# A branch hint, an earlier flag read and stores by thirds at the end of a fused RWKV and SwiGLU kernel

## The chip, the core and the metric

The kernel runs on one core of a Trainium2 chip. A core has five engines that work side by side: TensorE (PE, matrix products; its weight loads are listed as PEld), VectorE (DVE), ScalarE (ACT), GpSimd (POOL) and SyncE (SP, which here only issues transfers and waits). Each engine runs its own instruction queue in order; the queues meet through semaphores. The metric is device time in microseconds, and the median over several executions is what counts.

## The reference

The program computes two things in a row, in float32. The first is a linear attention with a decaying state; the second is a gated feed-forward layer on its output. Shapes: batch 4, 8 heads, 768 steps, head size 48; then 3072 tokens of 384 values, with an inner size of 1536.

```python
for t in range(S):
    kt, vt, rt = (k[:, :, t], v[:, :, t], r[:, :, t])
    cur = np.einsum('bhd,bhe->bhde', u[None] * kt, vt)
    y[:, :, t] = np.einsum('bhd,bhde->bhe', rt, state + cur)
    state = w[None, :, :, None] * state + np.einsum('bhd,bhe->bhde', kt, vt)
...
g = x @ w_gate                       # x: y as (3072, 384)
silu = g * (1.0 / (1.0 + np.exp(-g)))
val = x @ w_val
return silu * val @ w_out
```

## The kernel before, in words

The program holds two whole implementations. `fast` is correct as long as all decay rates `w` lie in a range that its tables of powers can hold; `general` works for any `w`. `fast` runs first and always to its end. On the way (step 12 of its main loop) it counts the entries of `w` outside the range into one integer in on-chip memory, `outside`. The outermost function then reads that integer into a register of every engine (line 1360) and branches (line 1361): if it is over zero, `general` computes everything again and overwrites the output. With the data used here the count is zero, so every engine jumps over the whole of `general`, whose instructions lie between the branch and the end of the program. Behind the branch stand the closing waits: SP waits for every outstanding transfer and every engine, and a barrier over all engines ends the program (put down to line 1755).

`fast` handles 24 blocks of 128 tokens. The attention of a block and the feed-forward of earlier blocks are interleaved by a hand-written order (`todo`, `feed`), and the kernel is built with a manual schedule, so program order on each engine is the order in which the Python code issues. The feed-forward is done for groups of blocks. For the last two groups of four blocks, called by their first pair's number as `THREES` = 8 and `THREES + 2` = 10, the products go through a scheme that multiplies 3 x 3 blocks by 2-column blocks with 15 products instead of 18: `three_units` for the gate and value products (line 787 issues their matmuls) and `project_thirds` for the output projection (line 1013). Everything that remains once the interleaved queue is empty is the list `tail`: the gate and value products of group 8, its projection, the same products of group 10, and its projection. The tail's first matmuls run at 429.8 us.

`project_thirds(g)` has 15 rounds, named r0 to r14 in the order of `THIRDS`, which ends with r2, r6, r9, r5, r11, r7. A round is one matrix product of eight matmuls (two token blocks q of 128 rows, four each) into a PSUM bank, followed by `evict`, which copies, adds or subtracts the bank into one or two of the six result pieces `c[0]` to `c[5]`. The pieces lie in `rows`, which holds, for each q, two output tiles j of 384 columns: piece k is columns 128 (k // 2) to 128 (k // 2) + 128 of tile j = k % 2. The last four rounds finish the pieces: r9 finishes c[4], r5 finishes c[0] and c[1], r11 finishes c[2] and c[3], r7 finishes c[5]. In the last group (`ends`) the two rounds r6 and r7 of the chain "l5" are `split`: each q has a bank of its own and is evicted on its own, on VectorE (line 1008).

`store(q, j)` (line 977) sends one output tile of 128 rows by 384 columns, 192 KB, to DRAM (line 981). It issues from ACT's queue, except in the last group for q = 0, where it issues from SP's. Each transfer raises one of eight counters in turn when it lands; a later transfer on the same counter first waits for the earlier one.

Of the kernel before, what the change touches and what calls it, by code (L numbers as in the profile page):

```python
# [15 lines left out]
P = 128  # L16
# [6 lines left out]
def fast(  # L23
# [24 lines left out]
    nc = tc.nc  # L48
# [7 lines left out]
    DM, DFF = moe_w_gate.shape  # L56
# [41 lines left out]
    def take():  # L98
        return free.popleft()
# [170 lines left out]
    for e in range(2):  # L270
# [3 lines left out]
        out=ub.rearrange("p h d -> p (h d)"),  # L274
        in_=bass.AP(tensor=u.tensor, offset=u.offset, ap=[[0, P], [1, H * D]]),
# [9 lines left out]
    def warm(n):  # L285
# [9 lines left out]
        out=mask[:], in_=mask[:], compare_op=ALU.is_gt, fill=0.0,  # L295
# [11 lines left out]
    for l in range(7):  # L307
        n = 1 << l
# [449 lines left out]
    def prepare_threes(g, n):  # L758
        if n == 6:
            x_forms(g)  # L760
        for _ in range(2):
            if todo_x:
                todo_x.popleft()()
        if g > THREES:
            return
        if n == 1:
            if g == FIRST:
                todo_forms.extend(in_place(0) + in_place(1))
            if g == THREES:
                todo_forms.extend(w_forms(g, 1))  # L770
        if n == 7:
            todo_forms.extendleft(reversed(w_forms(g, 0)))
        for _ in range(2):
            if todo_forms:
                todo_forms.popleft()()
# [127 lines left out]
    def third(x, k, j):  # L903

        return x[:, :, 4 * k : 4 * k + 4, P * j : P * j + P]
# [39 lines left out]
    def project_thirds(g):  # L945

        ends = g + 2 == N // 2
        A, B_, C, D_, E, F = room["h"]
        (x00, x01), (x10, x11), (x20, x21) = (
            [third(hTs, k, j) for j in range(2)] for k in range(3)  # L950
        )
        h = {
            "r3": A, "r4": B_, "r1": C, "r0": D_, "r8": E, "r10": F, "r14": A, "r13": B_,
            "r12": C, "r2": D_, "r6": E, "r5": x00, "r7": x21, "r9": x20, "r11": x11,
        }
        rows = hv[:, NR + 6 : NR + 12].rearrange("p (q r) t -> p q (r t)", q=2)
        c = [rows[:, :, DM * (k % 2) + P * (k // 2) :][:, :, 0:P] for k in range(6)]
        made = {
            0: [(dve.tensor_sub, E, x01, x11)],
            1: [(dve.tensor_add, F, x01, x21)],  # L960
            2: [(dve.tensor_add, A, x10, x20)],
            3: [(dve.tensor_sub, B_, x00, F)],
            4: [(dve.tensor_add, C, B_, x20)],
            5: [(dve.tensor_sub, D_[q], D_[q], x20[:, q]) for q in range(2)],
            6: [(dve.tensor_add, E[:, q], D_[q], x21[:, q]) for q in range(2)],
        }
        used = {
            "r3": [("copy", 2)], "r4": [("copy", 1)], "r1": [("copy", 0)], "r0": [("sub", 2)],
            "r8": [("copy", 3), ("sub", 1)], "r10": [("copy", 5)], "r14": [("copy", 4)],
            "r12": [("add", 0)], "r13": [("add", 4)], "r2": [("add", 5)], "r6": [("add", 3)],  # L970
            "r9": [("sub", 4)], "r5": [("sub", 0), ("sub", 1)], "r11": [("add", 2), ("add", 3)],
            "r7": [("add", 5)],
        }
        lasts = ("r4", "r0", "r8", "r9", "r5", "r11", "r7")
        open_ = {}

        def store(q, j):
            cc, b = divmod(2 * (g + q) + j, B)
            n0 = S * b + P * cc
            issue = sp if ends and q == 0 else act  # L980
            issue.dma_start(out=out[n0 : n0 + P, :], in_=rows[:, q, DM * j : DM * j + DM])

        def make(n):
            for op, o, a, b in made.get(n, ()):
                op(o, a, b)
            if not ends:
                prepare_threes(g + 2, n)

        def item(n):
            what, chain = THIRDS[n]  # L990
            if n:
                make(n)
            first = chain not in open_
            split = ends and chain == "l5"
            if first:
                open_[chain] = [take()] + ([ring_a.popleft()] if split else [])
            banks_ = open_[chain]

            def evict(q):
                for how, k in used[what]:  # L1000
                    x = banks_[0][:, 0 : 2 * P].rearrange("p (q t) -> p q t", q=2)
                    if split:
                        x = banks_[q][:, q * P : q * P + P]
                    o = c[k][:, q] if split else c[k]
                    if how == "copy":
                        act.copy(o, x)
                    else:
                        (dve.tensor_add if how == "add" else dve.tensor_sub)(o, o, x)

            for q in range(2):  # L1010
                ps = banks_[q if split else 0][:, q * P : q * P + P]
                for f in range(4):
                    pe.matmul(  # L1013
                        ps, (h[what][q] if h[what] is D_ else h[what][:, q])[:, f, :], wide["o"][what][:, f, :],
                        start=first and f == 0 and (split or q == 0), stop=f == 3, skip_group_check=True,
                    )
                if split:
                    evict(q)
                    if what == "r7":
                        store(q, 1)  # L1020
            if not split:
                evict(None)
            if n == 0:
                for do in wide.pop("last"):
                    do()
                make(0)
            if what in lasts:
                free.append(banks_[0])
            if what == "r11":
                store(0, 0)  # L1030
                store(1, 0)
            if what == "r7" and not split:
                store(0, 1)
                store(1, 1)
        return [lambda n=n: item(n) for n in range(15)]

    def three_units(g):
# [225 lines left out]
    for s in range(4, N + 2):  # L1263
# [3 lines left out]
        if s + 2 == SWAPPED:  # L1267
# [3 lines left out]
            for p, o in ((slice(0, 64), 64), (slice(64, P), -64)):  # L1271
                sp.dma_start(
                    out=halves_of[p], in_=scales[p.start + o : p.stop + o, 1:3, H // 2 : H]
# [68 lines left out]
    tail = threes[0] + projections[0][:-2]  # L1342
    tail += threes[1][0:1] + projections[0][-2:-1] + threes[1][1:2] + projections[0][-1:]
    tail += threes[1][2:] + projections[1]
    for piece in tail:
        piece()


@with_exitstack
def kernel(  # L1350
    ctx: ExitStack,
    tc: tile.TileContext,
    *args: bass.AP,
):
    nc = tc.nc
    ctx.enter_context(tc.manual_schedule())
    flag = ctx.enter_context(tc.tile_pool(name="flag", bufs=1))
    outside = flag.tile([1, 1], INT32, name="outside")
    fast(tc, *args, outside[:])
    n = nc.values_load(outside[:], min_val=0, max_val=512)  # L1360
    with tc.If(n > 0):
        general(tc, *args)


# [395 lines left out]
```

## Time and profile before

| what | us |
|---|---|
| median of 5 runs | 596.67 |
| lowest and highest of them | 595.38 and 597.52 |
| the profiled execution's own time | 595.54 |
| its span, first to last instruction | 593.8 |
| start of the tail on PE | 429.8 |
| last store issued | 588.1 |
| SP's waits for stores end | 592.2 |

The span is the time from the first to the last instruction of the program; the execution's own time is a little longer, since it holds what the runtime does around it. Busy times are sums per engine, and engines overlap. A wait names the engine that waits, the line, and who released it. The granted TensorE clock in this execution was 0.999 of full speed. A q behind an engine's name means an entry of its instruction queue that is not arithmetic: a transfer's issue, a semaphore wait, a register load, a branch.

### The profile page before, as it was taken

How to read it: one execution, taken by the hardware profiler on the slowest of the kernel's cores; microseconds unless marked ns; L12 is line 12 of the kernel's file. 1: busy time of each engine (PE TensorE's matmuls, PEld its weight loads, DVE VectorE, ACT ScalarE, POOL GpSimd, SP SyncE). 2: the span in 40 equal slices, each digit the busy share in tenths (PEclk: the TensorE clock that was granted, in tenths of full speed). 3: DMA queues.
4: the chain of work that ended last, by engine and by line, in shares of the span. 5: the costliest groups of instructions: out<-in, count | busy, mean ns of one | idle time of the engine just before them, and what ended most of it. 6: DMA issues, size and time to landing. Idle time of an engine off the chain costs nothing.

```text
span 593.8 us, 13239 instructions
## 1 busy us (share of the span) xinstructions
PE 580.6 (98%) x5240; PEld 522.5 (88%) x5240; DVE 421.5 (71%) x702; ACT 225.2 (38%) x516; POOL 355.5 (60%) x378
## 2 busy tenths in 40 slices
PE   8899999999999999999999999999999999999995
PEld 7688888899888899988899988889988899988895
DVE  5977877488488877478787477779257878377672
ACT  3468886221443422244431344423134320233310
POOL 5889879999999502977600996513678960010600
PEclk9999999999999999999999999999999999999999
DMA  7989896952342333233234233200100000100001
GB/s 160 254 220 249 219 298 88 84 80 46 78 75 31 50 54 66 49 54 63 41 57 79 68 53 57 47 13 3 54 1 1 1 1 1 55 0 1 1 2 59
DMA packets 148151, 41.73 MB, mean 70 GB/s; under 512 B 138480, under 2 KB 141936, under 8 KB 148080
## 3 DMA queue, kind: packets, MB, share of 16 engines
q1 hardware_dynamic: 144912, 36.47, 31.1%
q10 hardware_dynamic: 3168, 4.33, 2.0%
q8 instruction: 43, 0.70, 0.5%
q14 instruction: 28, 0.23, 0.1%
HBM read 28.51 MB, written 4.72 MB: 56 GB/s over the span
## 4 chain that ended last, share of the span: by engine, by line
PE 88%; POOL 3%; DVE 2%; issue 1%; ACT 1%; POOLq 0%
PE bank L787 31%; PE bank L606 18%; PE ring L787 13%; PE bank L1013 9%; PE bank L531 7%; PE ring L493 6%; PE ring L440 3%; POOL wgv L242 1%; PE ring L508 1%; DVE hv L811 1%; POOL hats L332 0%; POOL rk L254 0%; POOL hats L329 0%; PE ring L371 0%; POOL rk L255 0%
## 5 line engine op out<-in xcount | busy, mean ns | idle before, releaser
L811 DVE TENSOR_TENSOR hv<-hv,bank 128x512 f32<-128x512 f32 x132 | 87.2, 682 | 25.7 <-PE bank L787 14.6
L531 PE MATMUL bank<-xT,wgv 128*128 128x256 f32 x288 | 66.5, 384 | 0.6 <-ACT xT L497 0.6
L787 PE MATMUL bank<-xf,wgv 128*128 128x256 f32 x256 | 65.9, 382 | 0.0
L350 ACT ACTIVATE At<-ident,du 128x128 f32<-128x128 f32 x176 | 59.9, 398 | 15.0 <-DVE du L260 6.6
L811 ACT COPY hv<-bank 128x512 f32<-128x512 f32 x72 | 40.2, 586 | 58.3 <-PE bank L787 51.9
L531 PEld LDWEIGHTS bank<-xT,wgv 128*128 128x128 f32 x288 | 53.3, 190 | 8.9 <-ACT xT L497 0.9
L717 POOL TENSOR_TENSOR s<-wgv 128x256 f32<-128x256 f32 x39 | 29.9, 791 | 48.6 <-PE bank L606 48.5
L787 PEld LDWEIGHTS bank<-xf,wgv 128*128 128x128 f32 x256 | 47.8, 190 | 7.0 <-DVE kT L1055 0.6
L1064 POOL TENSOR_TENSOR hv<-At,hats 128x512 f32<-128x512 f32 x8 | 10.2, 1274 | 65.9 <-ACT At L1063 65.9
L818 ACT ACTIVATE hv<-hv 128x512 f32<-128x512 f32 (+1 forms) x33 | 21.2, 668 | 45.9 <-DVE hv L811 45.9
L521 POOL TENSOR_TENSOR Z<-Z,w 48x192 f32<-48x192 f32 x32 | 16.9, 528 | 35.7 <-DVE Z L520 34.5
L493 PE MATMUL ring<-At,v_ld 128*32 128x128 f32 x768 | 34.9, 273 | 1.4 <-DVE At L450 1.4
L787 PE MATMUL bank<-xT,wgv 128*128 128x256 f32 x144 | 35.9, 382 | 0.3 <-DVE hv L811 0.3
L787 PE MATMUL bank<-xT,s 128*128 128x256 f32 x152 | 35.3, 380 | 0.0
L606 PE MATMUL bank<-wt,hs 128*128 128x192 f32 x192 | 33.7, 328 | 0.6 <-DVE hs L580 0.6
L606 PE MATMUL bank<-wo,hs 128*128 128x192 f32 x192 | 33.9, 327 | 0.0
L606 PE MATMUL bank<-wo,hv 128*128 128x192 f32 x192 | 33.4, 327 | 0.0
L787 PEld LDWEIGHTS bank<-xT,s 128*128 128x128 f32 x152 | 28.6, 190 | 4.5 <-issue 0.8
L606 PEld LDWEIGHTS bank<-wt,hs 128*128 128x128 f32 x192 | 31.3, 190 | 1.4 <-ACT At L350 0.8
L493 PEld LDWEIGHTS ring<-At,v_ld 128*32 128x32 f32 x768 | 30.3, 110 | 2.5 <-DVE At L450 2.2
L606 PEld LDWEIGHTS bank<-wo,hv 128*128 128x128 f32 x192 | 31.6, 190 | 0.4
L606 PEld LDWEIGHTS bank<-wo,hs 128*128 128x128 f32 x192 | 31.6, 190 | 0.3
(220 smaller groups left out, 1401.0 us busy)
## 6 DMA issues: line engine op xcount, KB each, us to landing
hats<-hats SPq DMA_DIRECT2D x192, 32.0 KB, 2.0
w_bits<-in_moe_w_gate_dram SPq DMA_DIRECT2D x6, 768.0 KB, 6.5
w_bits<-in_moe_w_val_dram SPq DMA_DIRECT2D x6, 768.0 KB, 5.8
w_bits<-in_moe_w_out_dram SPq DMA_DIRECT2D x6, 768.0 KB, 6.5
out_dram<-hv ACTq DMA_DIRECT2D x22, 192.0 KB, 2.0
v_ld<-in_v_dram SPq DMA_DIRECT2D x24, 96.0 KB, 5.6
k_ld<-in_k_dram SPq DMA_DIRECT2D x8, 192.0 KB, 3.9
r_ld<-in_r_dram SPq DMA_DIRECT2D x8, 192.0 KB, 4.1
```

Source lines behind the costliest of these rows:

```text
L350: lambda h=h: act.activation(At[i % 2][:, h, :], ident[:], AF.Identity, scale=du[:, h : h + 1])
L440: pe.matmul(ps[e][keys, a, cols], kT[i % 2][rows, at(i, a), keys], turned[i][rows, at(i, a), cols], start=True, stop=True, skip_group_chec ...
L493: pe.matmul(ps[32 * q : 32 * q + 32, cc, :], *x, start=start, stop=stop, skip_group_check=True,)
L521: pool.tensor_mul(ze, ze, w)
L531: pe.matmul(gv[:, o, :].rearrange("p (i t) -> p i t", i=2), wt[:, c, P * f : P * (f + 1)], xT[:, 2 * g % NX : 2 * g % NX + 2, c, :], start ...
L606: pe.matmul(ps, lhs[:, f, :], rhs[:, f, :], start=(f == 0 and n in (0, 1, 4)), stop=(f == FH - 1), skip_group_check=True,)
L717: op(made[o], made[a], made[b])
L787: pe.matmul(ps[:, o], u[:, o], v, start=first and o == 0, stop=True, skip_group_check=True,)
L811: do(out, *(pair_of(wide[a][:]) if isinstance(a, str) else a for a in args))
L818: todo.append((at, lambda: act.activation(gate, gate, AF.Silu)))
L1013: pe.matmul(ps, (h[what][q] if h[what] is D_ else h[what][:, q])[:, f, :], wide["o"][what][:, f, :], start=first and f == 0 and (split or ...
L1064: todo.append((muls, lambda: on.tensor_mul(h, sg, value)))
```

## The change

Three things are changed.

First, the read of `outside` into registers moves from behind `fast` to a place inside it, ahead of the tail. `fast` returns the register value and the outermost function only branches on it.

Second, next to that read, `mark_branch_hint_location("general", engines=all)` puts one hint instruction on each engine that announces the coming branch, which carries the same label. The hint says that the branch is likely taken.

Third, in the last group (`ends`) an output tile is no longer stored whole. `store` takes a slice of columns, and `whole` names, for each of the last four rounds, the pieces that it finishes; `store_thirds` stores those pieces, 128 rows by 128 columns each, right behind the round's eviction. Stores for q = 0 still issue from SP and those for q = 1 from ACT. The twelve stores of 64 KB stand where four of 192 KB stood. The earlier group keeps its four whole stores.

```diff
-        def store(q, j):
+        def store(q, j, o=slice(0, DM)):
             cc, b = divmod(2 * (g + q) + j, B)
             n0 = S * b + P * cc
             issue = sp if ends and q == 0 else act
-            issue.dma_start(out=out[n0 : n0 + P, :], in_=rows[:, q, DM * j : DM * j + DM])
+            issue.dma_start(
+                out=out[n0 : n0 + P, o], in_=rows[:, q, DM * j + o.start : DM * j + o.stop]
+            )
+
+        whole = {"r9": (4,), "r5": (0, 1), "r11": (2, 3), "r7": (5,)} if ends else {}
+
+        def store_thirds(q, what):
+            for k in whole.get(what, ()):
+                store(q, k % 2, slice(P * (k // 2), P * (k // 2) + P))
...
                 if split:
                     evict(q)
-                    if what == "r7":
-                        store(q, 1)
+                    store_thirds(q, what)
...
-            if what == "r11":
+            if not split:
+                for q in range(2):
+                    store_thirds(q, what)
+            if what == "r11" and not ends:
                 store(0, 0)
                 store(1, 0)
-            if what == "r7" and not split:
+            if what == "r7" and not ends:
                 store(0, 1)
                 store(1, 1)
...
     tail += threes[1][2:] + projections[1]
+    n = nc.values_load(outside, min_val=0, max_val=512)
+    tc.mark_branch_hint_location("general", engines=list(mybir.ALL_ENGINES))
     for piece in tail:
         piece()
+    return n
...
-    fast(tc, *args, outside[:])
-    n = nc.values_load(outside[:], min_val=0, max_val=512)
-    with tc.If(n > 0):
+    n = fast(tc, *args, outside[:])
+    with tc.If(n > 0, label="general"):
         general(tc, *args)
```

## The prediction

> **What bounds the kernel now.** I read the page's busy rows first, then the chain that ended last, then the last 8 us by line, and last the place where the moved instructions will stand, at 430 us. The busy rows and the chain say that TensorE is the clock of the whole program:
>
> ```profile
> span 593.8 us, 13239 instructions
> ...
> PE 580.6 (98%) x5240; PEld 522.5 (88%) x5240; DVE 421.5 (71%) x702; ACT 225.2 (38%) x516; POOL 355.5 (60%) x378
> ```
>
> The chain over the last 14 us, in order of time (start, length, what), shows where TensorE lets go:
>
> ```profile
> 586.84 0.91 PE ring L1013 x8
> 587.75 0.02 issue
> 587.77 0.29 DVE hv L1008
> ```
>
> VectorE's last addition ends at 587.77 + 0.29 = 588.06, but the span ends at 593.8. So 5.7 us run after the last arithmetic, and only there can this change gain. The answers for line 1360 (the flag's read) and line 1361 (the branch and what follows it) give engine, duration and start. A trailing q means the engine's instruction queue:
>
> ```profile
> L1360 PEldq TENSOR_LOAD <-outside x1: 488/488/488, 585.6 to 585.6; - x1
> L1360 SPq TENSOR_LOAD <-outside x1: 767/767/767, 587.6 to 587.6; - x1
> L1360 DVEq TENSOR_LOAD <-outside x1: 930/930/930, 587.8 to 587.8; - x1
> ...
> L1360 ACTq TENSOR_LOAD <-outside x1: 482/482/482, 588.5 to 588.5; - x1
> ```
>
> ```profile
> L1361 SPq EVENT_SEMAPHORE  x8: 17/17/17, 591.6 to 592.2; - x8
> ...
> L1361 PEldq COMPARE_BRANCH  x1: 3718/3718/3718, 586.2 to 586.2; - x1
> ...
> L1361 DVEq COMPARE_BRANCH  x1: 72/72/72, 588.8 to 588.8; - x1
> L1361 SPq COMPARE_BRANCH  x1: 45/45/45, 588.8 to 588.8; - x1
> L1361 ACTq COMPARE_BRANCH  x1: 54/54/54, 589.0 to 589.0; - x1
> ...
> L1361 ACTq EVENT_SEMAPHORE  x1: 17/17/17, 592.8 to 592.8; - x1
> L1361 DVEq EVENT_SEMAPHORE  x1: 21/21/21, 592.8 to 592.8; - x1
> ```
>
> The reader is to see the hole after each branch. PE's branch itself lasts 3.7 us. SP, DVE and ACT branch in 45 to 72 ns, but their next instruction comes 2.8, 4.0 and 3.8 us later. The page also counts instruction packets (q8: 43 for 0.70 MB, 16 KB each; q14: 28 for 0.23 MB, 8 KB each). I read the hole as the wait for the code behind the branch, which jumps over the whole general path. The SP queue's own waits in the last 14 us say who is last:
>
> ```profile
> SPq L1361 <- SPq L1361: 2.8, 1, 2.8
> SPq L1755 <- PEq L1755: 0.6, 2, 0.5
> SPq L1755 <- DVEq L1361: 0.3, 1, 0.3
> ```
>
> SP leaves its hole at 591.6, passes eight waits for stores (to 592.2), and in the second row of waits stands 0.3 us for DVE, which is still in its own hole. So two things end nearly together: the last store (issued at 588.1, landing 3.1 us later in the answer for line 981, so at 591.2) and the holes of DVE and ACT (592.8). The holes win by 1.6 us. Taking them away exposes the store.
>
> **The change part by part.**
>
> *The flag's read moved to the head of the tail.* It removes from the end the loads above (0.48 to 0.93 us) and on SP the two register instructions behind its load (192 and 33 ns). ACT's branch moves from 589.0 to just behind its store issue, 588.1 + 0.34 = 588.5; DVE's from 588.8 to about 588.1; SP's from 588.8 to about 587.6. It puts the same instructions on all five queues where the tail starts, which the timeline has at 429.8 on PE:
>
> ```profile
> 429.48 0.40 PE L493 MATMUL ring<-At,v_ld 128*32 128x128 f32 x8
> 429.82 1.99 PE L787 MATMUL ring<-xf,wgv 128*128 128x256 f32 x8
> ```
>
> Queue by queue. SP: its last load before the tail is issued at 384.6 to 388.5 and its next DMA is at 586.4; covered. DVE: idle 5.91 us before its first operation there (434.5); covered, and 0.93 us would still fit. ACT: a copy starts at 429.98 and the next at 430.98, with 0.53 us of waiting on PE between; a 0.48 us load that runs beside the copy fits, without that cover 0.5. POOL: its tail starts at 427.55 and it is busy 41.6 of the 50.2 us up to 480, but no wait of PE on POOL appears from 429.8 on; covered. PE is the one with no cover. From the load's start (585.6) to the branch (586.2) its queue was held 0.6 us; with a hint of some 0.05 (the 51 ns of a PE semaphore instruction is the nearest row), 0.65. Low end: at the kernel's end PE's queue ran ahead of the array (the load at 585.6 stands behind matmuls that start up to 587.5), and with such a lead the loss is 0. High end: no lead, and the longest load of the five, 0.93 + 0.1 + 0.05 = 1.1. The matmuls before 429.8 are the short 32-column ones, four of them running at a time and every instruction issued in nanoseconds, and weight loading there shows a gap of 0.20 us put down to issue. That speaks for little lead. I take a loss of 0.4, and since PE is the chain from there to 587.75, it goes into the total whole.
>
> *The hint itself.* Five instructions in the same place; no row of before has one. Between 17 ns (a semaphore instruction on SP or ACT) and 0.5 us (a load that runs out to memory); 0.05 is in the 0.65 above and the 1.1 bounds it. What it should do is to have the branch's target fetched while the tail runs 158 us. If it does, each hole shrinks to about the branch's own 45 to 72 ns; at worst it stays at 2.8 to 4.0.
>
> *The last stores by thirds.* Before: four stores of 192 KB, two after r11 and two after r7. After: twelve of 64 KB, two after r9 (about 582.8), four after r5 (585.0), four after r11 (586.7), two after r7. Six issues each on SP and ACT at 0.34 to 0.38 us: 2.1 us on each queue over 5.3. ACT's last copy of the tail is at 573.5 and SP does nothing else, so no arithmetic waits behind them. A store's issue can wait for an older landing on the same counter, of which there are eight in turn: the twelfth waits for the fourth, issued by 585.4. At 1.9 to 2.6 us it has landed by 588.0 (covered by the 588.1 issue), at the 4.1 us of the present last stores it would come at 589.5 and cost 1.0; I take nothing and keep that in the upper end. VectorE's writes beside columns that are being stored: the earlier triple has the same pattern (strided r7 result beside a running store at 510.7) and there VectorE waited for PE only. No wait added.
>
> The landing of the last store sets the end. Bounds: 1.9 us (192 KB stores from ACT at 418 to 428, and equally the 0.8 KB load of w) and 3.1 us (as now, with 768 KB issued within 1.7 us). In the last 1.7 us there will be 384 KB instead, and the last piece has the queues nearly to itself; I take 2.2, nearer to the quiet rows.
>
> The Trainium skill, page "DMA: Bandwidth & Descriptors", section "Anatomy of one DMA", speaks against the thirds: it gives a DMA a fixed cost of about 2.0 us whatever its size, mostly the confirmation of the last byte. Worked out from that page as an estimate, 64 KB instead of 192 KB would save 0.3 us of 2.4, and landing would be 2.0 + 0.15 = 2.15 instead of 2.2, so the sum would move by 0.05; the rows at 1.9 are already below the page's 2.0, and no run shown here has a 64 KB store to DRAM.
>
> *Sum against the profiled execution* (595.54 us: span 593.8 and 1.7 around it). The last store is issued at 588.1 + 0.4 = 588.5 and lands at 590.7. Behind it SP has one or two more store waits (0.1), then from the first wait of line 1755 to the end 593.8 - 592.2 = 1.6 less the 0.3 spent on DVE, so 1.3. The span ends at 590.7 + 1.4 = 592.1, 1.7 less than now. ACT's and DVE's branches lie at 588.9 and 588.5 and are done by 589.0; SP's hole, even if it stayed (588.0 + 2.8 = 590.8, 8 waits to 591.4, then 1.3), would give 592.7. Profiled time 595.54 - 1.7 = 593.8. The median of the five runs, 596.67, is 1.13 above that execution, so I forecast 596.67 - 1.7 = 595.0.
>
> **The rivals.**
>
> *The hint doesn't act* (wrong side of the branch, or target not kept). The holes stay and only the loads go: ACT branches at 588.5 + 0.4 = 588.9 instead of 589.0, so 0.1 less in all: 596.6. For it: no row of before shows a hint working. Against it: every engine's branch is taken to a target that it then waits for, which is the plain case.
>
> *The last store takes over at its present landing.* 588.5 + 3.1 = 591.6, + 1.4 = 593.0, a gain of 0.8: 595.9. For it: all four last stores now take 3.1 to 4.1, so something there slows them, and code packets for five engines will still move near them. Against: half the bytes.
>
> *Slower: the fetch for the hint takes the place of the next block on TensorE.* PE's 43 packets of 16 KB over 594 us are one every 14 us, so the tail crosses about 11 of them. If the early target fetch once pushes out the block that PE is about to run, PE pays the 3.7 us of its branch row in mid-tail. Against the gain of 1.7 that is 2.0 net: 598.7. It decides from one stall of more than 1.7 us. For it: PE has no slack. Against: the trace of before shows PE stalled on code only at the branch.
>
> **How the numbers follow.** Forecast case 0.60, hint idle 0.14, present landing 0.13, stall on PE 0.13. The predicted time is the first: 595.0, its own range from loss 0 and landing 1.9 (588.1 + 1.9 + 1.4 = 591.4, 2.4 less, 594.3) to loss 1.1 with landing 3.1 (593.7, 0.1 less, 596.6). The five runs spread by 2.1 us, so a median may be off by 0.4: 593.9 to 597.0. That holds all but the stall, and the other two cases lie inside. I put the low end at 593.7, since the 1.7 us outside the span hold code fetches too. A measurement of this kernel tells about 0.2% from nothing, 1.2 us: the forecast's 1.7 is just past that, so 0.57 faster (the first case nearly whole), 0.28 same (both smaller gains and the rest of the first), 0.15 slower (the stall, and an idle hint with a PE loss near 1.1).
>
> **What would show it.** Right: next instructions of DVE and ACT within 0.5 us of their branches, PE's branch under 0.3 us, SP last waiting for a DMA, about 592 as the end. PE's loss is the shift of the first L787 matmul behind L493's last from 0.34 us to about 0.7. Wrong: holes of 3 to 4 us again, or a PE gap of 3 us between 430 and 588, or landings of the last piece above 3 us.

## The result and the profile after

The changed kernel takes 595.3 us (median of 39 runs) against 596.28 us (median of 67 runs of the kernel before, which are more than the five shown ahead). The ratio is 0.9982, with a 95% interval of 0.9975 to 0.9989: a gain of 1.1 us, between 0.7 and 1.5. The forecast was 595.0 from 596.67, a gain of 1.7. So the sign is right, the size is two thirds of what was forecast, and the gain is just under the 0.2% that the prediction took as the least that counts. That 595.3 lies so near 595.0 is in part luck: over 67 runs the median of the kernel before came out 0.4 us lower than over the first five.

The page and the chain of the last 14 us, of the changed kernel:

```profile
span 593.7 us, 13258 instructions
...
PE 580.7 (98%) x5240; PEld 522.0 (88%) x5240; DVE 422.3 (71%) x702; ACT 225.4 (38%) x516; POOL 355.6 (60%) x378
```

```profile
587.60 0.91 PE ring L1021 x8
588.51 0.02 issue
588.53 0.29 DVE hv L1016
```

The span looks unchanged (593.7 after 593.8), but that is two unlike parts. VectorE's last addition ends at 588.82 here and at 588.06 before, so everything ahead of it is 0.76 us longer in this one execution; behind it there are 4.88 us instead of 5.75. The first part is spread between executions, not the change: the changed kernel profiled a second time (below) has that addition end at 587.74, 1.1 us earlier than here, and over all the kernels below it ends anywhere from 587.7 to 589.6. Most of the 0.76 comes at two places, about 0.6 between 362 and 374 us and 0.4 at 519 us, where nothing was edited. I therefore read all experiments by two numbers: the ratio of the times, and the stretch from VectorE's last addition to the end of the span in the one profiled execution, called the *end stretch* from here on. It has a spread too: the two kernels that were profiled twice gave 4.88 and 4.41, and 4.70 and 5.04. A difference under 0.5 us between two profiles is therefore not told from chance.

The branch and what follows it (line 1373 of the changed kernel; engine, duration, start):

```profile
L1373 SPq EVENT_SEMAPHORE  x8: 17/17/17, 590.1 to 592.3; - x8
...
L1373 PEldq COMPARE_BRANCH  x1: 402/402/402, 586.3 to 586.3; - x1
...
L1373 DVEq COMPARE_BRANCH  x1: 84/84/84, 588.5 to 588.5; - x1
L1373 DVEq EVENT_SEMAPHORE  x1: 21/21/21, 589.2 to 589.2; - x1
L1373 SPq COMPARE_BRANCH  x1: 70/70/70, 589.6 to 589.6; - x1
L1373 ACTq COMPARE_BRANCH  x1: 68/68/68, 589.6 to 589.6; - x1
L1373 ACTq EVENT_SEMAPHORE  x1: 17/17/17, 590.1 to 590.1; - x1
```

The holes are gone. PE's branch takes 0.40 us (3.72 before), and the next instruction of DVE, SP and ACT comes 0.5 to 0.6 us after the branch (2.8 to 4.0 before). But SP and ACT branch only at 589.6. Counted from VectorE's last addition that is 1.0 us (SP) and 0.4 us (ACT) later than in the run "PE held" below, where no late store issue is long. SP's eight store waits reach to 592.3. The reason stands in the stores (line 981 of the changed kernel, last 14 us: duration as min/median/max in ns, starts, and the times to landing of all twelve):

```profile
L981 SPq DMA_DIRECT2D out_dram<-hv x6: 332/374/1437, 583.6 to 589.2; - x6
L981 ACTq DMA_DIRECT2D out_dram<-hv x6: 348/390/1397, 583.6 to 589.2; - x6
...
DMA to landing us min/median/max: 1.7/2.2/4.2
```

```profile
SPq L981 <- DVE hv L1016: 164.6, 4, 160.5
SPq L1373 <- SPq L1373: 2.3, 3, 1.6
SPq L1767 <- PEq L1767: 0.6, 2, 0.5
```

One issue on SP and one on ACT, both of them behind r11 at 587.6 to 587.7, took 1.4 us instead of 0.35, and both ended at 589.06. So the two stores behind r7 were issued at 589.15, though their data were ready at 587.93 and 588.82. Then they needed 2.9 and 3.1 us to land, where the six stores up to 586 needed 1.7 to 1.9. The second fence (SP's waits) shows SP waiting three times behind its branch, 1.6 us at the longest (it ends at 591.88, as the long-issued store of ACT lands at 591.87), and no longer for DVE: the row "SPq L1755 <- DVEq L1361" of before has no successor.

The hint and the flag's read are at other places than the source suggests (lines 1767 and 1355):

```profile
L1767 SPq BRANCH_PREFETCH_HINT  x1: 56/56/56, 0.8 to 0.8; - x1
...
L1767 PEldq BRANCH_PREFETCH_HINT  x1: 50/50/50, 0.9 to 0.9; - x1
```

```profile
L1355 PEldq TENSOR_LOAD <-outside x1: 627/627/627, 429.5 to 429.5; - x1
L1355 ACTq TENSOR_LOAD <-outside x1: 472/472/472, 430.4 to 430.4; - x1
```

The mark stands ahead of the tail in the Python code, but the instruction was put at the start of the program's block, at 0.8 us. The read is where it was written.

### The profile page after: what moved, and what is told of

It is laid out like the page before. It is cut to its first block, busy times and chain, and to the rows that moved or that the text cites. A ratio compares the mean times of both kernels' runs of the same rounds, so it can differ in the third digit from the quotient of the medians.

```text
span 593.7 us, 13258 instructions
## 1 busy us (share of the span) xinstructions
PE 580.7 (98%) x5240; PEld 522.0 (88%) x5240; DVE 422.3 (71%) x702; ACT 225.4 (38%) x516; POOL 355.6 (60%) x378
## 4 chain that ended last, share of the span: by engine, by line
PE 84%; POOL 4%; SPq 3%; DVE 1%; issue 1%; ACT 1%; DMA 0%; POOLq 0%; DVEq 0%
PE bank L787 28%; PE bank L606 18%; PE ring L787 13%; PE bank L1021 9%; PE bank L531 7%; PE ring L493 5%; PE ring L440 3%; SPq L397 2%; POOL wgv L242 1%; PE ring L508 1%; POOL hats L332 1%; SPq L141 1%; SPq L148 1%; POOL rk L254 0%; POOL hats L329 0%
```

## The experiments

Theory A was the prediction's: the hint empties the holes, and then the last store's landing ends the program. Its rivals were B, that the thirds carry the gain, and C, that the early read does. Four runs first took the three parts of the change apart.

**Hint and early read, whole stores.** The changed kernel without the third part:

```diff
-                    store_thirds(q, what)
+                    if what == "r7":
+                        store(q, 1)
...
-            if not split:
-                for q in range(2):
-                    store_thirds(q, what)
-            if what == "r11" and not ends:
+            if what == "r11":
```

> Hint and early read as in the change, the last stores whole as before (four of 192 KB). Theory A (the hint empties the holes behind the branches, and what then ends last is the landing of the last store, slowed on one DMA engine by code blocks that are fetched behind the branches): the last store is issued 0.03 us after VectorE's last addition and not held up, lands 3.0 to 3.2 us later, and the span ends 1.4 us after that; 1.0 to 1.5 us less than before. Theory B (the thirds carry the gain, since a smaller last store lands sooner): without them at most 0.5 us less than before.

Measured: ratio 0.9997 (0.9984 to 1.001), 0.2 us less than before, end stretch 4.70 us. The last store is issued 0.03 us behind VectorE's last addition and lands 3.2 us later, as theory A said. The time did not come as theory A said: it fits theory B's "at most 0.5", and theory A's 1.0 lies just outside the interval. The run was repeated below, and the repeat fits theory A.

**The thirds alone.** The kernel before with the third part only.

```diff
-            if what == "r11":
-                store(0, 0)
-                store(1, 0)
+            if not split:
+                for q in range(2):
+                    store_thirds(q, what)
```

> The thirds alone: the flag is read at the end as before and no hint is given. Theory A: DVE's and ACT's holes of 3.8 to 4.0 us still end last, so no more than 0.2 us either way, and if anything slower where the twelve issues hold ACT past its branch. Theory B: 0.5 us less or more.

Measured: ratio 1.0013 (1.0001 to 1.0025), end stretch 6.74 us, 1.0 longer than before (in an execution of 598.03 us, 1.7 above this kernel's median, so the 1.0 may be more than is usual). Theory B falls as to the thirds by themselves: alone they are a loss, 0.8 us by the ratio. The branch rows of this run show how:

```profile
L1371 DVEq COMPARE_BRANCH  x1: 72/72/72, 589.9 to 589.9; - x1
L1371 ACTq COMPARE_BRANCH  x1: 54/54/54, 591.2 to 591.2; - x1
L1371 SPq COMPARE_BRANCH  x1: 45/45/45, 591.6 to 591.6; - x1
```

VectorE ends at 589.56 here. An issue of 1.73 us on SP and one of 0.98 on ACT hold these two queues until 590.6; only then come the read and the branch, and the hole of 2.9 us starts 1.6 us (ACT) and 2.0 us (SP) behind VectorE's end, where before it was 1.0 and 0.7. Theory A had expected a loss of this kind but not its size.

**The hint alone.** Whole stores, flag read at the end.

```diff
+    tc.mark_branch_hint_location("general", engines=list(mybir.ALL_ENGINES))
     for piece in tail:
         piece()
...
-    with tc.If(n > 0):
+    with tc.If(n > 0, label="general"):
```

> The hint alone: whole stores, the flag read at the end. Theory A: the loads of 0.5 to 0.9 us end before the last store lands, so it is within 0.2 us of the run with hint and early read: 0.9 to 1.5 us less than before. Rival C (the early read is what pays, since it takes 0.5 to 0.9 us from the end of every queue): half of that at most, 0.6 us less.

Measured: ratio 0.9987 (0.9978 to 0.9997), end stretch 5.04 us, 0.7 less than before. The holes are gone here as in the changed kernel, with nothing but the hint added:

```profile
L1362 DVEq COMPARE_BRANCH  x1: 84/84/84, 589.3 to 589.3; - x1
L1362 DVEq EVENT_SEMAPHORE  x1: 21/21/21, 589.9 to 589.9; - x1
```

The hint by itself makes the kernel faster, by 0.8 us, just under theory A's 0.9; rival C's bound of 0.6 lies inside the interval (0.2 to 1.3 us), so this run alone does not exclude C.

**The early read alone.**

```diff
     tail += threes[1][2:] + projections[1]
+    n = nc.values_load(outside, min_val=0, max_val=512)
     for piece in tail:
         piece()
+    return n
```

> The early read alone: whole stores, no hint. Theory A: the holes stay and start 0.55 us earlier on ACT, 0.7 on DVE, so 0.5 us less than before if the read costs PE nothing at 430 us (first wide matmul still 0.20 us behind the last narrow one); 0.0 to 0.1 if PE loses 0.4 there, as the prediction's term had it. Rival C: 0.9 us less or more.

Measured: ratio 0.9996 (0.9985 to 1.0007), end stretch 5.30 us, 0.45 less than before. The holes stay:

```profile
L1362 DVEq COMPARE_BRANCH  x1: 72/72/72, 588.3 to 588.3; - x1
L1362 DVEq EVENT_SEMAPHORE  x1: 21/21/21, 591.7 to 591.7; - x1
```

The 0.45 is near theory A's 0.5 with no loss on PE, but within the spread of two profiles; the time shows no difference that it could tell. Rival C's 0.9 us lies at the very end of the interval and far from the profile, so C does not carry the gain. PE's matmuls around the read at 430 us, here and in the changed kernel, in that order:

```profile
430.03 0.40 PE L493 MATMUL ring<-At,v_ld 128*32 128x128 f32 x8
430.37 1.35 PE L787 MATMUL ring<-xf,wgv 128*128 128x256 f32 x5
```

```profile
429.87 0.41 PE L493 MATMUL ring<-At,v_ld 128*32 128x128 f32 x8
430.21 1.56 PE L787 MATMUL ring<-xf,wgv 128*128 128x256 f32 x6
```

The first wide matmul starts 0.34 us behind the start of the last narrow group, as before (429.82 - 429.48). A read of 0.63 us in PE's queue costs PE nothing: it begins at 429.46, while the array still works off narrow matmuls, the last of which starts at 430.01.

What holds up the last stores was now the open question. The trace also has the records of the DMA packets, and among them those of the two instruction queues: in the changed kernel PE's block of 16 KB starts at 587.70, 1.36 us behind its branch, takes 0.97 us, and lies just on the issues of 1.4 us; the other engines' blocks of 8 KB come at 590.17, 590.69 and 590.77, on the landing of the last two stores. In the kernel before, PE's block starts at 587.20 and lies on the four stores as well. Queue, packets, MB and busy share of the two instruction queues (q8 for PE's 16 KB, q14 for the 8 KB of the others) from 582 us on, in the kernel before and in the changed one, in that order:

```profile
q14 instruction: 6, 0.05, 1.3%
q8 instruction: 2, 0.03, 1.1%
```

```profile
q14 instruction: 3, 0.02, 0.8%
q8 instruction: 1, 0.02, 0.5%
```

So the hint takes half of these fetches away and leaves the other half. The Trainium skill, page "Runtime: NRT & Kernel Launch", section "Instruction fetch mechanics", says that an engine fetches its next page of code over a DMA queue of its own while it executes the current one. The packets behind each branch agree as far as the trace goes: they come on queues apart from those of the stores, but all engines other than PE stand under the one number q14. Theory D: these blocks hold up the stores' transfers. Theory E: the stores crowd each other.

**No branch, whole stores.** The flag's read, the branch and the general path are left out.

```diff
-    n = nc.values_load(outside[:], min_val=0, max_val=512)
-    with tc.If(n > 0):
-        general(tc, *args)
```

> The flag's read, the branch and the whole general path are left out (the data's decay rates lie inside the range, so the output doesn't need them); four whole stores. Theory D (code blocks fetched by TensorE and the others around the branch hold up one DMA engine, and this is what makes the last stores land 3.1 to 4.2 us after their issue): without the far jump no code fetch of 16 KB falls between 585 and 590 us unless a block ends there anyway; the last store lands 1.9 to 2.1 us after its issue, all four under 2.7, and the span ends at most 3.6 us after VectorE's last addition (before: 5.7). Theory E (the last stores crowd one another: 768 KB within 1.7 us): the last of them still lands 2.8 us or more after its issue.

Measured (one execution): 593.58 us, end stretch 2.81 us. The last code packet starts at 578.04. The four stores land 2.6, 2.4, 2.2 and 1.9 us after their issue (4.1, 3.8, 3.5 and 3.1 before, with the same bytes in the same time). Theory D holds, E falls for the larger part: crowding is at most the difference from 1.9 to 2.6, the code blocks that from 1.9 to 3.1.

The counters of the stores show how the delay looks. A store raises its counter in sixteen steps, one as each of its sixteen parts lands. In the kernel before, fifteen parts of the last store have landed 1.90 us after its issue, just as without the branch (all sixteen by 1.88), and only the sixteenth comes at 3.08. The same can be seen far from any branch. Of the 192 transfers of 32 KB on line 397 in the kernel before, 36 had a 16 KB code block in flight during the first 1.9 us. They land after 2.99 us (median), the other 156 after 1.97, and the fifteenth part comes at the same time in both (1.97 and 1.95). Over 2.5 us are 28 of the 36 and 4 of the 156. Nine of the 36 issues took over 1 us, none of the 156 did. So a 16 KB code block as a rule holds up one part in sixteen, and sometimes an issue; it need not come from a branch.

**No branch, thirds.** The same, with the third part of the change.

> The same without read, branch and general path (left out), but with the last stores by thirds. Theory D: no store's issue lasts over 0.5 us, the last landing comes 1.6 to 1.9 us after its issue, and the end is 0.1 to 0.3 us nearer to VectorE's last addition than with whole stores. Theory E: issues of 1 us or more remain (twelve transfers fill the queues).

Measured (one execution): 592.06 us, end stretch 2.48 us. Line 981 in its last 14 us, to be held against the same rows of the changed kernel above:

```profile
L981 SPq DMA_DIRECT2D out_dram<-hv x6: 332/374/398, 582.7 to 587.2; - x6
L981 ACTq DMA_DIRECT2D out_dram<-hv x6: 338/366/449, 582.7 to 587.9; - x6
...
DMA to landing us min/median/max: 1.5/1.7/1.9
```

The same twelve issues take 0.45 us at most. The last store lands 1.54 us after its issue, where the whole one took 1.88, and the end stretch is 0.33 us shorter (0.03 more than expected). So the thirds do what they should once nothing fetches code beside them, as far as one execution of each kernel shows it. The skill's page "DMA: Bandwidth & Descriptors", section "Anatomy of one DMA", which the prediction weighed, has the difference right (an estimate of 0.3 from its bandwidth). Its fixed part of 2.0 us is too high for these stores, which both land below it; that section is written for DMAs that GpSimd issues, and these are issued by SP and ACT.

**PE held.** To move PE's code block, the changed kernel got one more matmul of one element that waits for VectorE's last result.

```diff
     for piece in tail:
         piece()
+    last = hv[:, NR + 6 : NR + 12].rearrange("p (q r) t -> p q (r t)", q=2)
+    pe.matmul(take()[0:1, 0:1], last[:, 1, 767:768], last[:, 1, 767:768], start=True, stop=True)
     return n
```

> The changed kernel, and PE gets one more matmul of one element that reads VectorE's last result, so that PE's branch comes 2 us later (588.5 us after the start instead of 586.3) and its fetch of 16 KB with it. Theory D: the store issues at r11 and r7 take 0.33 to 0.45 us (1.4 in the changed kernel), the last store is issued 0.05 us after VectorE's last addition, and the end comes 0.4 to 1.2 us nearer to it than the 4.9 us of the changed kernel. Theory E: issues of 1.4 us and an end within 0.2 us of 4.9.

Measured (one execution): end stretch 5.15 us, so the gain that theory D gave for it is missing. Its first half came true: the issues behind r11 and r7 take 0.40 us or less, and the last store is issued 0.03 us behind VectorE's end. But the block then falls on the last store (packets at 589.53, 589.65, 589.95 and 590.18; the third is PE's, 1.39 us long):

```profile
L981 ACTq DMA_DIRECT2D out_dram<-hv x1: 338/338/338, 588.7 to 588.7; - x1
...
DMA to landing us min/median/max: 3.7/3.7/3.7
```

Thirteen of the sixteen parts of that store had landed 1.58 us after the issue, about as without a branch (1.54 for all sixteen); the last three came at 2.31, 2.92 and 3.66. So again most parts are on time and a few are late, here three with four blocks in flight, and theory D has to be widened only to more than one part. That a late part and a block share one of the sixteen DMA engines is the likely reading; the records don't name the engine, so it is not shown.

**All three held.** ACT and VectorE each overwrite one column of the piece sent by the store before the last, which makes them wait for its landing; PE reads VectorE's column.

```diff
     for piece in tail:
         piece()
+    last = hv[:, NR + 6 : NR + 12].rearrange("p (q r) t -> p q (r t)", q=2)
+    act.copy(last[:, 0, 640:641], ident[:, 0:1])
+    dve.memset(last[:, 0, 767:768], 0.0)
+    pe.matmul(take()[0:1, 0:1], last[:, 0, 767:768], last[:, 0, 767:768], start=True, stop=True)
     return n
```

> The changed kernel, and behind the tail ACT and VectorE each overwrite one column of the piece that the store before the last has sent (so they wait for its landing), and PE multiplies VectorE's column: all three branch about 1 us after the last store's issue, SP as before. Theory D: the last store's transfer meets at most SP's fetch of 8 KB and lands 1.6 to 2.0 us after its issue; the end comes 3.3 to 3.8 us after VectorE's last addition (4.9 in the changed kernel), 2.0 to 2.5 us less than before in time. Theory E: 4.7 us or more.

Measured: ratio 0.9968 (0.9955 to 0.998), 1.9 us less than before, end stretch 3.48 us. The last store, issued 0.03 us behind VectorE's end:

```profile
L981 ACTq DMA_DIRECT2D out_dram<-hv x1: 339/339/339, 588.7 to 588.7; - x1
...
DMA to landing us min/median/max: 2.0/2.0/2.0
```

Three instructions added in front of the branch, and waits for a landing with them, shorten the end by 1.4 us against the changed kernel (0.9 against its second run below): what moved is when code is fetched. The 1.9 us (1.2 to 2.7) are just under the 2.0 that theory D gave. E, which asked for 4.7 us or more, has no room for this.

**The last four, on one chip.** The changed kernel again, whole stores again, all held with whole stores, and all held with the last SP store moved to ACT's queue:

```diff
-            issue = sp if ends and q == 0 else act
+            issue = sp if ends and q == 0 and (j, o.start) != (1, 2 * P) else act
```

> The changed kernel once more, beside the next three. Theory D: again TensorE's block of code (fetched 1.2 to 1.4 us behind its branch) falls among the stores of r11 and r7, one or both of the issues behind it last over 1 us, and the end comes 4.6 to 5.1 us after VectorE's last addition; 0.8 to 1.4 us less than before. If the long issues were chance, 0.4 us each and an end at 4.4 or less.

> Hint and early read with whole stores once more, on the same chip as the changed kernel. Theory D (beside the code fetches the thirds gain nothing: more transfers wait behind the block): end 4.6 to 4.9 us after VectorE's last addition and a time within 0.4 us of the changed kernel's on either side. Theory B: 0.5 us or more above it.

> All three branches held as in the run with thirds, but with the four whole stores. Theory D: with the fetches out of the way a whole last store lands 0.3 us after a third does (as in the two runs without a branch, 1.88 against 1.54): end 3.7 to 4.0 us after VectorE's last addition (3.5 with thirds), time 1.3 to 1.8 us less than before. If a whole store can't be kept clear of the fetches: 4.3 or more.

> All three held, thirds, and the store before the last moved from SP's queue to ACT's, so that SP branches 0.4 us earlier and its fetch of 8 KB (at 589.53, 0.8 us behind the last store's issue) ends before the last store's packets. Theory D: the last landing goes from 1.98 to 1.6 us, the end to 3.1 to 3.3 us after VectorE's last addition; 2.0 to 2.6 us less time than before. If SP's fetch is harmless, the same 3.5 as with SP.

Measured, with all runs in one table (the last landing is counted from that store's issue):

| kernel | ratio to before (95%) | end stretch, us | longest issue, us | last landing, us |
|---|---|---|---|---|
| before | 1 | 5.75 | 0.38 | 3.1 |
| changed | 0.9982 (0.9975 to 0.9989) | 4.88 | 1.44 | 3.1 |
| changed, again | 0.9991 (0.9982 to 1.0) | 4.41 | 1.68 | 2.4 |
| hint and read, whole stores | 0.9997 (0.9984 to 1.001) | 4.70 | 1.14 | 3.2 |
| the same, again | 0.998 (0.9969 to 0.999) | 5.04 | 1.37 | 3.3 |
| thirds alone | 1.0013 (1.0001 to 1.0025) | 6.74 | 1.73 | 3.2 |
| hint alone | 0.9987 (0.9978 to 0.9997) | 5.04 | 0.37 | 3.6 |
| read alone | 0.9996 (0.9985 to 1.0007) | 5.30 | 0.38 | 2.8 |
| no branch, whole stores | one execution | 2.81 | 0.38 | 1.9 |
| no branch, thirds | one execution | 2.48 | 0.45 | 1.5 |
| PE held | one execution | 5.15 | 0.44 | 3.7 |
| all held, thirds | 0.9968 (0.9955 to 0.998) | 3.48 | 0.44 | 2.0 |
| all held, whole stores | 0.9979 (0.9968 to 0.9989) | 3.90 | 0.38 | 2.4 |
| all held, SP early | 0.9971 (0.9959 to 0.9983) | 3.49 | 0.45 | 1.9 |

The long issues come back in the changed kernel (1.68 and 1.64 us, PE's block at 586.47 among them), so they are no accident, though its end stretch was 0.2 under the range given, and its gain, 0.5 us, under the 0.8 given. What the thirds are worth beside the fetches stays open within about a microsecond. On the one chip that had both kernels, whole stores were 0.7 us faster by the ratios, which excludes theory B's 0.5 us slower there and is more than the 0.4 given. The first pair of ratios (0.9982 and 0.9997) points the other way by 0.9 us, and the end stretches mix (4.4 and 4.9 against 4.7 and 5.0). With the branches held, the end stretch is 0.42 us shorter with thirds than with whole stores. That is near the 0.3 of the kernels without a branch, but no more than two profiles of one kernel differ by; the times, 0.9968 and 0.9979, don't part them. Moving SP's last store to ACT brought nothing (3.49, where 3.1 to 3.3 was expected): SP's block came earlier, at 589.19, and then held up the other store behind r7 (2.4 us), on whose landing ACT, DVE and PE wait.

The kernel with all three held is the fastest with the output computed in the same way and the general path in place: 1.9 us under before, 0.8 under the first measurement of the changed kernel. Against the changed kernel on time alone that is not fully settled (0.9955 to 0.998 beside 0.9975 to 0.9989), the profile's end stretch is clearer (3.5 against 4.4 and 4.9).

## Why the prediction came out as it did

**That the holes behind the branch end last, and that the hint empties them: right.** Rows of before gave it, the changed kernel's branch rows confirm it, and the hint alone is faster. A branch whose target is there costs 0.4 to 0.6 us up to the next instruction, not the 45 to 72 ns of the branch's own row that I took for the forecast; it lies beside the store's landing and costs nothing. The signs that I gave for it, 0.5 us on DVE and ACT and under 0.3 on PE, are missed narrowly on DVE (0.60) and PE (0.40).

**The term "PE loses 0.4 at 430 us": wrong, it is 0.** I read the gap of 0.20 us put down to issue as a sign that PE's queue had no lead. The gap is there with the read and without, so it comes with the step from narrow to wide matmuls and is no sign of an empty queue. The lead at that place was about half a microsecond (read started at 429.46, last narrow matmuls at 430.01). The hint's 0.05 within this term isn't even there, but at 0.8 us; the rival in which it drives PE's next block out in mid-tail did not occur.

**The term "no wait for the last issue": wrong by 0.3 us.** The last store was issued 0.33 us behind VectorE's end, where I had 0.04. I looked for the wait at the eight counters. It came from the issue ahead of it on the same queue, which lasted 1.4 us. The row was in the trace of before, at 511 us: 768 ns for one ACT issue, in the same rows of line 981 as the 338 ns ones, and I used the median. A 16 KB code block was in flight there too (510.84 to 511.91).

**The term "the last store lands in 2.2 us": wrong, 3.1.** This is the failing size, and "landings of the last piece above 3 us" was one of my own signs of being wrong (3.08 measured). I named the upper bound of 3.1 and explained it by 768 KB of crowding. The runs without a branch show that crowding is not it (1.9 for the same stores); code fetched around the branch is. With the hint only half of these fetches go, the rest still come about 1 us behind each branch, and my second rival ("code packets for five engines will still move near them") had this in a half sentence. What happened is that rival's case without the loss on PE: 588.1 + 3.1 + 1.4 = 592.6, a gain of 1.2, against 1.1 measured.

**The term "1.4 us from the landing to the end": right.** Landing at 592.24, end of the span at 593.70: 1.46.

The sum: from VectorE's last addition to the end I had 0.04 + 2.2 + 1.4 = 3.6 us, and 4.9 was measured; 0.3 of the difference is the issue, 0.9 the landing. The 0.4 for PE was an error the other way, so the forecast gain should have been 0.8 too high by these terms; it was 0.6 too high (1.7 against 1.1), which the interval of the measured gain (0.7 to 1.5) allows. The thirds, which I counted on for the step from 3.1 to 2.2, bring nothing in this kernel that these runs can tell, and are a loss without the hint.

## What to carry to other kernels

A far branch at a kernel's end costs more than its own wait: code is fetched behind it, and the stores that were in flight at that time here landed 0.8 to 2.4 us late and could hold an issuing queue for a microsecond. The hint took the wait away but only half of the fetches, so look at when each engine reaches the branch, and let the engines that are done early wait until the last store is on its way. And a bound of "as slow as now" should be explained before a smaller value is taken: here the explanation (too many bytes) was wrong, and the smaller value with it.

## What was not expected of the hardware

- A hint of 50 ns at 0.8 us still served its branch 585 us and, on PE, some forty blocks of code later. No code packet was recorded between it and 17 us, so the traces don't show when the target was fetched or where it was kept.
- A DMA issue, 0.34 us as a rule, can take up to 1.7 us while code is being fetched, but need not: both issues behind r7 in the kernel before (587.23 to 587.59 and 588.09 to 588.43) lie within PE's block (587.20 to 588.43) and take 0.36 and 0.34 us. The two long issues on SP and ACT ended together (589.06 in the changed kernel), which suggests that the two queues wait for something in common.
- Without a branch the end stretch with whole stores is 2.8 us instead of 5.7, in one profile each: the branch over code that never runs costs about 2.9 us there. The version with all branches held and stores by thirds is at 3.48, 2.3 us under before, with the general path in place.
